# Attention followed by a two-layer MLP on one core: the MLP in two phases, with seven products in both GEMMs

## The chip, the cores and the metric

One core of one Trainium2 chip runs the whole program. The metric is device time in microseconds (us) of one execution; the kernel before has a median of 611.99 us over 3 runs (611.94 to 612.11).

The engines are named as in the profile: PE is TensorE (PEld its weight loads), DVE is VectorE, ACT is ScalarE, POOL is GpSimd, SP is SyncE, which issues most DMAs. PSUM is the memory that PE writes, in eight banks; SBUF is the other on-chip memory; DRAM is off the core.

## What is computed

```python
def _attn_ref(q, k, v):                      # q, k, v: (4, 12, 448, 64) float32
    scores = (1.0 / np.sqrt(64)) * np.matmul(q, k.transpose(0, 1, 3, 2))
    scores = np.where(np.triu(np.ones((448, 448), dtype=bool), k=1), -1e9, scores)
    attn = np.exp(scores - scores.max(-1, keepdims=True))
    return np.matmul(attn / (attn.sum(-1, keepdims=True) + 1e-9), v)

def _moe_ref(x, w_in, w_out, alpha):         # x: the 1792 tokens x 768 of attention
    h = x @ w_in                             # w_in 768 x 2048, float64
    g = np.maximum(h, 0.0) + alpha * np.minimum(h, 0.0)
    return (g @ w_out).astype(np.float32)    # w_out 2048 x 768, float64
```

The two weight matrices arrive as float64. The kernel reads them as pairs of 32-bit words and makes float32 values of them on the chip ("decode"). To keep float32 accuracy on PE, every GEMM operand is split into a high part (a cast to the fp32r type) and a low part (value minus high part), and each product is three matmuls: high by high, high by low, low by high.

## The kernel before, in words

**Attention (0 to about 147 us).** 24 pairs of heads go through a software pipeline; `ORDER` (line 38) lists the steps of one round and how many rounds each lags behind. PE does scores, transposes of the probabilities and the product with v. Decoding for the first group of the MLP is put into the rounds by the table `EARLY` (line 25). The output of each pair is split into a high part, which stays in SBUF (`xw`, `xp`), and a low part, which is stored in DRAM (`lows`, line 184) and loaded again whenever a GEMM step needs it (`load_low`, line 666).

**MLP (about 147 us to the end).** The 2048 hidden features are worked off in 8 groups `g` of 256 (two chunks of 128), the tokens in two blocks `bp` of 2 x 384 and 2 x 512; a (group, block) is a "quad". For each quad the first GEMM makes four PSUM tiles (2 chunks x 2 halves of the tokens). In group 0 that is 12 plain steps of 6 matmuls. In the other groups (`STEPS`, line 642) 4 of the 6 chunks of the inner dimension 768 go through a Strassen-Winograd scheme with 7 products in place of 8 (P1 to P7; sums S1 to S4 of weight blocks, T1 to T4 of token blocks), and the last 2 chunks are added plainly (LX, LY, LZ, LW): 11 steps of 6 matmuls (`h_mms`, line 686; the matmul is line 694). Then `h_act` (line 727) applies the activation, `g_hi` and `g_lo` (lines 748, 755) split the result, and `o_part` (line 783; matmul line 793) does the second GEMM for the same quad at once, plainly: for each tile of 128 tokens and each half of 384 output columns 6 matmuls into one bank, which DVE adds to an accumulator in SBUF (line 798). The second GEMM of quad q-1 is interleaved with the first GEMM of quad q. PE's stream alternates between both GEMMs, so that whatever one waits for, the other covers.

**Decode, per piece of 128 x 384 values** (64 pieces: 32 of w_in, 32 of w_out): ACT absolute value (line 251), POOL clamp (254), four DVE operations (257, 261, 264, 265), POOL add (268). Weight sums S1 to S4 are line 273, casts to the high part lines 295 and 325, low parts on POOL lines 299 and 328.

**What sets the order.** Each engine runs its instructions in program order. The order around the GEMMs is written out by hand in the tables `FIRST`, `SECOND`, `CYCLE` and `LATER` (lines 46 to 115), `PER` (line 117) and `low_calls` (line 935). SP issues all loads of pieces and low parts in order.

## Time and profile before

| | |
|---|---|
| median of 3 runs | 611.99 us |
| span of the profiled execution, first to last instruction | 609.8 us |
| what lies around the span (median less span; the page shows no time of its own for that execution) | 2.2 us |
| PE busy | 603.9 us, 99% |
| DVE, POOL, ACT busy | 507.1, 391.9, 284.5 us |
| instructions | 10958 |
| bytes moved by DMA | 120.40 MB |

How to read it: "busy" is the time in which an engine executed, including time in which an executing instruction was held up inside it. Matmuls overlap in the pipeline, so the mean duration of one matmul is longer than the distance from one to the next; the distance is read from the chain of work, which merges runs of matmuls. "PEclk" is the granted TensorE clock; 9 in the page and 1.00 in a table of stretches are full speed, the 2.4 GHz level.

### The profile page before, as it was taken

To read this page: it belongs to the slowest core of one execution; us is meant where nothing else is said; L and a number is where in the kernel's file an instruction comes from. 1 tells how busy PE (TensorE), PEld (TensorE's weight loads), DVE (VectorE), ACT (ScalarE), POOL (GpSimd) and SP (SyncE) were. 2 spreads that over 40 slices of the span, in tenths; PEclk is the share of its full clock that TensorE was granted. 3 is DMA by queue.
4 is the path that set the end of the run, shared out by engine and by line. 5 is a ranking of instruction groups with operands and counts; after the bars stand their busy time and mean duration, and the time that the engine had idled before them with its cause. 6 is when DMAs were issued, how large, how long until landed. Compare 5 with 4: busy or idle time off the path is not lost.

```text
span 609.8 us, 10958 instructions
## 1 busy us (share of the span) xinstructions
PE 603.9 (99%) x3533; PEld 528.3 (87%) x3533; DVE 507.1 (83%) x1123; ACT 284.5 (47%) x781; POOL 391.9 (64%) x531
## 2 busy tenths in 40 slices
PE   8999999999999999999999999999999999999997
PEld 4676767667879999999999899999999998999897
DVE  5999999998977778988897889878897978896364
ACT  6989989897656743333232313232332323231110
POOL 7766687867485669756874776487568747762120
PEclk9999999999999999999999999999999999999999
DMA  7765477644885598657747756576577467554825
GB/s 171 215 182 160 135 208 221 194 130 121 288 293 155 146 311 264 195 165 229 230 155 228 233 173 205 184 251 194 164 235 231 156 219 238 166 179 118 273 104 181
DMA packets 88105, 120.40 MB, mean 197 GB/s; under 512 B 12400, under 2 KB 66000, under 8 KB 88048
## 3 DMA queue, kind: packets, MB, share of 16 engines
q1 hardware_dynamic: 87008, 117.97, 62.0%
q0 software_dynamic: 576, 1.18, 0.8%
q10 hardware_dynamic: 464, 0.56, 0.3%
q8 instruction: 28, 0.46, 0.3%
q14 instruction: 29, 0.24, 0.1%
HBM read 105.00 MB, written 14.68 MB: 196 GB/s over the span
## 4 chain that ended last, share of the span: by engine, by line
PE 97%; DMA 1%; DVE 1%; POOL 0%; issue 0%; ACT 0%; POOLq 0%; DVEq 0%
PE o L793 38%; PE heldY L694 11%; PE heldX L694 8%; PE a L500 7%; PE pt L481 7%; PE s L425 6%; PE heldZ L694 6%; PE s L417 3%; PE heldW L694 3%; PE h_V L694 3%; PE h_Y L694 1%; PE h_X L694 1%; PE h_W L694 1%; PE h_Z L694 1%; DMA lo_T<-low_T 1%; PE warm L346 1%
## 5 line engine op out<-in xcount | busy, mean ns | idle before, releaser
L798 DVE TENSOR_TENSOR acc<-o,acc 128x384 f32<-128x384 f32 (+1 forms) x197 | 107.6, 550 | 64.1 <-PE o L793 63.4
L406 POOL TENSOR_SCALAR p<-p,rs 128x128 f32<-128x128 f32 (+3 forms) x164 | 81.2, 518 | 36.5 <-ACT ptf L402 22.0
L452 ACT ACTIVATE p<-s,nm 128x256 f32<-128x256 f32 (+3 forms) x168 | 81.9, 496 | 11.5 <-DVE nm L437 10.0
L437 DVE CUSTOM_DVE_ANT_0 s<-s,mask 128x128 f32<-128x128 f32 (+3 forms) x168 | 71.1, 481 | 9.1 <-PE s L425 5.2
L793 PE MATMUL o<-wo,g_Z 128*128 128x384 f32 (+1 forms) x339 | 76.9, 334 | 0.0
L793 PE MATMUL o<-wo,g_W 128*128 128x384 f32 (+1 forms) x339 | 76.7, 334 | 0.0
L793 PE MATMUL o<-wo,g_X 128*128 128x384 f32 x336 | 76.7, 336 | 0.0
L793 PE MATMUL o<-wo,g_Y 128*128 128x384 f32 x336 | 76.5, 335 | 0.0
L793 PEld LDWEIGHTS o<-wo,g_X 128*128 128x128 f32 x336 | 60.3, 188 | 2.0
L793 PEld LDWEIGHTS o<-wo,g_Z 128*128 128x128 f32 x339 | 60.5, 188 | 1.2
L793 PEld LDWEIGHTS o<-wo,g_W 128*128 128x128 f32 x339 | 60.3, 188 | 0.0
L793 PEld LDWEIGHTS o<-wo,g_Y 128*128 128x128 f32 x336 | 60.1, 188 | 0.0
L481 PEld LDWEIGHTS pt<-ident,p 128*128 128x128 f32 x384 | 43.3, 140 | 12.1 <-issue 7.7
L500 PEld LDWEIGHTS a<-ptf,v 128*64 128x64 f32 x384 | 25.4, 136 | 30.8 <-issue 11.2
L268 POOL TENSOR_TENSOR y_o<-y_o,x_o 128x384 f32<-128x384 f32 x32 | 33.4, 1045 | 25.9 <-DVE x_o L265 24.0
L481 PE MATMUL pt<-ident,p 128*128 128x128 f32 x384 | 47.1, 274 | 1.1 <-POOL p L406 1.0
L500 PE MATMUL a<-ptf,v 128*64 128x448 f32 (+3 forms) x384 | 46.8, 386 | 0.0
L268 POOL TENSOR_TENSOR y_i<-y_i,x_i 128x384 f32<-128x384 f32 x32 | 33.1, 1034 | 21.1 <-DVE x_i L265 18.7
L402 ACT ACTIVATE ptf<-pt 128x512 f32<-128x512 f32 (+1 forms) x71 | 37.4, 570 | 3.9 <-PE pt L481 3.8
L425 PE MATMUL s<-kr,qr 64*128 64x384 f32 (+2 forms) x288 | 38.7, 398 | 0.0
L753 ACT ACTIVATE g_Y<-t_Y 128x384 fp32r<-128x384 f32 (+1 forms) x16 | 9.3, 579 | 59.9 <-DVE t_Y L744 59.9
L254 POOL TENSOR_SCALAR x_i<-x_i 128x384 f32<-128x384 f32 x32 | 18.1, 567 | 29.3 <-ACT x_i L251 26.7
(189 smaller groups left out, 1360.1 us busy)
## 6 DMA issues: line engine op xcount, KB each, us to landing
lo_T<-low_T SPq DMA_DIRECT2D x28, 512.0 KB, 5.0
lo_B<-low_B SPq DMA_DIRECT2D x25, 512.0 KB, 4.8
raw_i<-in_moe_w_in_dram SPq DMA_DIRECT2D x32, 384.0 KB, 3.8
raw_o<-in_moe_w_out_dram SPq DMA_DIRECT2D x32, 384.0 KB, 3.7
lo_T<-low_T SPq DMA_DIRECT2D x28, 384.0 KB, 4.0
lo_B<-low_B SPq DMA_DIRECT2D x25, 384.0 KB, 4.0
lo_N<-low_N SPq DMA_DIRECT2D x16, 512.0 KB, 5.3
lo_N<-low_N SPq DMA_DIRECT2D x16, 384.0 KB, 4.3
```

The lines of the kernel that those rows point to most:

```text
L268: nc.gpsimd.tensor_tensor(out=y, in0=y, in1=xf, op=ALU.add)
L402: eng.activation(out, x, AF.Copy, scale=side)
L406: eng.tensor_scalar(out=out, in0=x, scalar1=side, scalar2=1.0, op0=ALU.mult, op1=ALU.mult)
L417: nc.tensor.matmul(ps, qd[p % 3], T["k", p], start=True, stop=True)
L425: nc.tensor.matmul(ps[:, o : o + lim], T["q", p][half(j), i * QP : (i + 1) * QP], T["k", p][half(j), :lim], start=(o == 0), stop=(n > 0 or ...
L437: nc.vector.tensor_tensor_reduce(out=t, in0=t, in1=masks[1] if i == NQ else masks[0][:, (NQ - 1 - i) * QP :], scale=-SCALE, scalar=MOST_F3 ...
L452: nc.scalar.activation(T["p", p, i][:, j, : t.shape[1]], t, AF.Exp, scale=-1.0, bias=T.pop(("nm", p, i, j)), accum_out=T["sm", p][:, z : z ...
L481: nc.tensor.transpose(ps[:, j - js[0], c], t[:, j, c * QP : (c + 1) * QP], T["ident"])
L500: nc.tensor.matmul(out[half(j), c * QP :], vs[b % 2][:, hp, c, j], x[:, c * QP : S], start=(c == 0), stop=(c == NQ),)
L694: nc.tensor.matmul(ps, w[:, u, k * P : (k + 1) * P], x, start=(first and i == 0), stop=(i == len(mms) - 1), skip_group_check=True,)
L793: nc.tensor.matmul(ps, x, w, start=(i == 0), stop=(i == 3 * GC - 1))
L798: nc.vector.tensor_tensor(out=a[:, cols], in0=ps, in1=a[:, cols], op=ALU.add)
```

## The change

The MLP is rewritten; attention keeps its rounds. What it does:

- **First GEMM for all tokens, then the second.** The activated result g (2048 x 1792 float32) is stored in DRAM (`gd`), and so is decoded w_out (`wd`). The second phase loads both back.
- **Seven products on all of both.** The first GEMM splits 768 into 2 x 3 chunks: 7 steps of 9 matmuls of 448 columns for each of 8 groups and 2 halves of the tokens, 1008 matmuls. The second pairs 4 chunks of the hidden dimension (`Q`, 4 of them) with 7 tiles `t` of 2 x 128 tokens: 28 tiles `q`, each 7 steps of 6 matmuls of 384 columns, 1176 matmuls. Before, there were 534 of 384 and 534 of 512 columns, and 1344 of 384.
- **Token operands stay in SBUF,** high and low parts. For tokens of the first half they are made during attention; for the second half T1 to T4 and B11 are kept or stored in float32, B21 and B22 come back from DRAM, and 18 casts and 18 subtractions (128 x 448) behind attention make their parts.
- **Decode with two DVE operations in place of four,** and one ACT operation more: ACT makes an integer of the low word, POOL adds integers.
- **In phase two** each tile needs 4 sums, 7 casts and 7 low parts of g (128 x 256), and each `Q` 8 sums, 14 casts and 14 low parts of w_out (128 x 384). The four output tiles are built by `ofork`, `keep`, `oz`, `evX`, `w22`, `evZ`, `evY`, and in `Q` 1 to 3 `e22`: on DVE 3 additions or copies from PSUM in `Q` 0 and 6 in the others, on ACT 4 and 2.
- **The order of both phases** is no table any more: a planner (`Plan`) lists the jobs with engines, assumed durations (`US`), room in buffers and due times, plays them through in Python when the program is built, and emits them in the order of their planned starts. Jobs marked "DVE|POOL" go to whichever is idle then, the first named first. On the chip each engine still runs its list in order.
- The last steps of group 0 stand in attention's tail: six steps of 9 matmuls, where before there were 14 of 6.

Core of the diff (the planner's loop, attention and the code of the removed tables left out):

```diff
+US = {
+    "abs": 0.56, "int": 0.56, "clamp": 0.62, "bits": 0.68, "add": 1.06, "cast": 0.53, "sum": {"DVE": 0.85, "POOL": 1.06}, "lo": {"DVE": 0.85, "POOL": 1.1},
+    "copy": 0.56, "psum": 0.66, "relu": 0.56, "act": 0.66, "step1": 1.8, "step2": 1.04, "issue": 0.35,
+    "out": 0.56, "take": 0.58, "gcast": 0.42, "gsum": {"DVE": 0.55, "POOL": 0.82},
+    "glo": {"DVE": 0.55, "POOL": 0.85},
+}
+LOAD, STORE = 4.0, 3.0
...
+STEPS = ["P1", "P5", "P6", "P2", "P7", "P3", "P4"]
+STEP = {
+    "P1": ("A11", "B11", "Y"), "P5": ("S1", "T1", "V"), "P6": ("S2", "T2", "Y"), "P2": ("A12", "B21", "X"),
+    "P7": ("S3", "T3", "Y"), "P3": ("S4", "B22", "Z"), "P4": ("A22", "T4", "Y"),
+}
...
+    def p_int(key):
+        ys[key] = rooms["y"].take()
...
+        nc.scalar.activation(ys[key].bitcast(I32), parts_of(key)[0], AF.Copy, scale=2.0**-29)
...
+    def p_shift(key):
+        x = xs[key].bitcast(I32)
+        ts(out=x, in0=x, scalar1=3, scalar2=0x3FFFFFF8, op0=ALU.logical_shift_left, op1=ALU.bitwise_and)
...
+    def p_add(key):
+        y, x = ys[key].bitcast(I32), xs[key].bitcast(I32)
+        nc.gpsimd.tensor_tensor(out=y, in0=y, in1=x, op=ALU.add)
...
+        mms = [m for k in range(KW) for m in ((0, k, xh), (1, k, xh))] + [(0, k, xl) for k in range(KW)]
+        for i, (u, k, x) in enumerate(mms):
+            nc.tensor.matmul(
+                ps, w[:, u, k * P : (k + 1) * P], x[:, k],
+                start=(st in ("P1", "P5") and i == 0), stop=(i == len(mms) - 1), skip_group_check=True,
             )
...
+    def h_relu(g, b, role):
+        t = tt[g, b, role] = rooms["t"].take()
+        nc.scalar.activation(t, bank_of(g, b, role), AF.Relu, scale=-1.0)
...
+        stt(out=t, in0=t, scalar=om[:, f : f + 1], in1=bank_of(g, b, role), op0=ALU.mult, op1=ALU.add)
...
+        nc.sync.dma_start(out=gd[f // 4][:, f % 4, n, b * S : (b + 1) * S], in_=t)
...
+                    job(("xh", nm, k), "ACT", "cast", lambda nm=nm, k=k: t_hi(1, nm, k, nc.scalar), of)
+                    job(("x", 1, nm, k), "DVE|POOL", "lo", lambda e, nm=nm, k=k: t_lo(1, nm, k, e), [("xh", nm, k)])
...
+        half_end = pl.named["P", NG - 1, 0, "P4"]
+        half_end["give"] += ["w"] * 14 + ["gset"] * 2 + ["wf"]
...
+            eng.tensor_tensor(out=g_of(q, nm), in0=g_of(q, x), in1=g_of(q, y), op=op)
...
+            nc.scalar.activation(gset[q][:, LEFT.index(nm), 0], g_of(q, nm), AF.Copy)
...
+            eng.tensor_tensor(out=t[:, 1], in0=g_of(q, nm), in1=t[:, 0], op=ALU.subtract)
...
+            for u in range(2):
+                x, w = gset[q][:, LEFT.index(an)], wo[Q, u, bn]
+                mms += [(x[:, h, u], w[:, l]) for h, l in ((0, 0), (0, 1), (1, 0))]
...
+        def o_plus(out, q, role, x):
+            nc.vector.tensor_tensor(out=out, in0=o_bank(q, role), in1=x, op=ALU.add)
...
+                job(
+                    ("gsum", q, nm), "DVE|POOL", "gsum", lambda e, nm=nm: g_sum(q, nm, e),
+                    [("gl", q)] + [("gsum", q, x) for x in of] + first, "gs" if nm == "S1" else "",
+                )
...
+                    ("glo", q, nm), "POOL|DVE", "glo", lambda e, nm=nm: g_lo(q, nm, e), [("gcast", q, nm)] + later,
...
+        for i in range(NQT * NTT // 2):
+            for st in STEPS:
+                for b in range(2):
+                    o_jobs(2 * i + b, st)
```

## Rows read from the trace of the kernel before

**Rows 1.** The page: busy time of each engine, and the chain that ended last

```profile
PE 603.9 (99%) x3533; PEld 528.3 (87%) x3533; DVE 507.1 (83%) x1123; ACT 284.5 (47%) x781; POOL 391.9 (64%) x531
...
PE 97%; DMA 1%; DVE 1%; POOL 0%; issue 0%; ACT 0%; POOLq 0%; DVEq 0%
```

**Rows 2.** Stretches: PE, PEld, DVE, ACT, POOL busy us (x instructions); clock, DMA share, GB/s

```profile
113.00:144.00 31.00, 31.00 (x234) 20.69 (x232) 29.25 (x109) 29.33 (x99) 22.62 (x47) 1.00 0.39 119
216.00:328.00 112.00, 112.00 (x602) 106.44 (x601) 97.42 (x161) 37.52 (x85) 78.76 (x89) 1.00 0.68 217
```

**Rows 3.** The chain in order of time: start us, us, what

```profile
183.40 20.83 PE o L793 x120
...
217.10 2.10 PE heldY L694 x12
...
240.11 2.75 PE heldY L694 x12
```

**Rows 4.** Groups by line and shape: xcount | busy us, mean ns | idle, releaser

```profile
L798 DVE TENSOR_TENSOR acc<-o,acc 128x384 f32<-128x384 f32 x195 | 106.9, 552 | 63.7 <-PE o L793 63.1
...
L328 POOL TENSOR_TENSOR wo<-y_o,wo 128x384 fp32r<-128x384 f32 x32 | 34.9, 1092 | 0.0
...
L268 POOL TENSOR_TENSOR y_i<-y_i,x_i 128x384 f32<-128x384 f32 x32 | 33.1, 1034 | 21.1 <-DVE x_i L265 18.7 <-PE heldX L694 2.5
...
L299 POOL TENSOR_TENSOR wi_A<-y_i,wi_A 128x256 fp32r<-128x256 f32 x25 | 21.1, 844 | 0.0
...
L261 DVE SCALAR_TENSOR_TENSOR y_i<-raw_i,x_i 128x384 int32<-128x384 int32 x32 | 20.3, 635 | 0.4
L257 DVE TENSOR_SCALAR x_i<-x_i 128x384 int32<-128x384 int32 x32 | 20.3, 634 | 6.6 <-POOL x_i L254 6.6
...
L254 POOL TENSOR_SCALAR x_i<-x_i 128x384 f32<-128x384 f32 x32 | 18.1, 567 | 29.3 <-ACT x_i L251 26.7 <-PE heldY L694 2.2
...
L251 ACT ACTIVATE x_i<-raw_i 128x384 f32<-128x384 f32 x32 | 17.8, 555 | 29.2 <-DMA raw_i<-in_moe_w_in_dram 29.1
...
L325 ACT ACTIVATE wo<-y_o 128x384 fp32r<-128x384 f32 x32 | 15.5, 511 | 0.8 <-PE a L500 0.8
...
L295 ACT ACTIVATE wi_A<-y_i 128x256 fp32r<-128x256 f32 x25 | 10.3, 412 | 0.3 <-POOL y_i L268 0.3
...
L402 ACT ACTIVATE xw<-acc 128x448 fp32r<-128x448 f32 x11 | 5.8, 582 | 0.0
...
L744 DVE SCALAR_TENSOR_TENSOR t_X<-heldX,t_X 128x512 f32<-128x512 f32 x7 | 4.8, 692 | 0.2
...
L725 ACT ACTIVATE heldY<-heldX 128x512 f32<-128x512 f32 x7 | 4.1, 581 | 26.4 <-PE heldX L694 26.4
...
L744 DVE SCALAR_TENSOR_TENSOR t_X<-heldX,t_X 128x384 f32<-128x384 f32 x7 | 3.9, 557 | 0.2
```

**Rows 5.** DVE in order of time, 300 to 330 us: start us, us, instruction

```profile
299.99 0.56 DVE L798 TENSOR_TENSOR acc<-o,acc 128x384 f32<-128x384 f32 x1 [1.13 <-PE o L793]
300.46 1.30 DVE L265 SCALAR_TENSOR_TENSOR x_o<-raw_o,x_o 128x384 f32<-128x384 uint32 x1
...
322.12 0.56 DVE L265 SCALAR_TENSOR_TENSOR x_o<-raw_o,x_o 128x384 f32<-128x384 uint32 x1
```

**Rows 6.** DVE in order of time, 180 to 184 us

```profile
182.83 0.42 DVE L273 TENSOR_TENSOR S<-y_i,y_i 128x256 f32<-128x256 f32 x1
```

**Rows 7.** POOL in order of time, 300 to 330 us

```profile
300.06 1.29 POOL L758 TENSOR_TENSOR g_X<-t_X,g_X 128x512 fp32r<-128x512 f32 x1 [0.31 <-ACT g_X L753]
...
304.11 0.73 POOL L299 TENSOR_TENSOR wi_A<-y_i,wi_A 128x256 fp32r<-128x256 f32 x1
```

**Rows 8.** DMA issues: xcount, KB each, median us from issue to landing

```profile
lo_T<-low_T SPq DMA_DIRECT2D x28, 512.0 KB, 5.0
...
raw_i<-in_moe_w_in_dram SPq DMA_DIRECT2D x32, 384.0 KB, 3.8
...
low_B<-low_B SPq DMA_DIRECT2D x16, 224.0 KB, 3.5
```

More of the change, by code (lines that the diff above doesn't have):

```diff
@@ L419, in scores @@
             return
-        banks = [bank(f"s_{p}_{n}_{j}") for j in range(2)]
+        banks = [bank("s", p, n, j, uses=2 - n) for j in range(2)]
         o = 0
@@ new lines, in t_lo, with t_both, t_four @@
+    def t_lo(h, nm, k, eng):
+        eng.tensor_tensor(
+            out=XL[h][nm][:, k], in0=x_f32(h, nm, k), in1=XH[h][nm][:, k], op=ALU.subtract
+        )
+    t_his, t_los, u_both = (
+        iter([(h, nm, k) for nm in names for k in range(KW)]) for h, names in ((0, TF), (0, TF), (1, ["B11"]))
+    )
+    t_fours = iter(range(KW))
+    def t_both(*x):
+        t_hi(*x, nc.scalar)
+        t_lo(*x, nc.vector)
+    def t_four():
+        k = next(t_fours)
+        nc.gpsimd.tensor_tensor(out=TF["T4"][:, k], in0=TF["T4"][:, k], in1=TF["T2"][:, k], op=ALU.subtract)
@@ L924, in scores_done, with pool @@
+    bits = {}
+    def pool(stack, name, side="left"):
+        return stack.enter_context(tc.tile_pool(name=name, bufs=1, side=side, reuse_waits="tile"))
+    more_s, late_s = ExitStack(), ExitStack()
     def scores_done():
         att_a.close()
-        for nm, n in (("t", 3), ("low", 4)):
-            gp[nm] = pool("m_" + nm, n, "right")
-        load_low(4)
+        more = pool(more_s, "more", "right")
+        more.tile([P, 8], F32, name="padr")
+        b11 = more.tile([P, 2, KW, S], F32R, name="b11")
+        wir = more.tile([P, 4, 2, NH], F32R, name="wir")
+        XH[1]["B11"], XL[1]["B11"] = b11[:, 0], b11[:, 1]
+        nc.sync.dma_start(out=b11[:, 1].bitcast(F32), in_=xd["B11"])
+        for i in range(4):
+            rooms["wi"].give(wir[:, i])
@@ new lines, with piece_jobs @@
+        left = {nm: len(x.free) for nm, x in rooms.items()}
+        pl = Plan(left, done)
+        job = pl.job
+        def piece_jobs(key, before, by=1e9):
+            k = ("add", key)
+            if k in done:
+                return
+            if ("load", key) not in done:
+                job(("load", key), "SP", "issue", lambda: p_load(key), (), "raw", lag=LOAD, by=by, behind=[("load", before)])
+            job(("abs", key), "ACT", "abs", lambda: p_abs(key), [("load", key)], "x", by=by, behind=[("abs", before)])
+            job(("clamp", key), "POOL", "clamp", lambda: p_clamp(key), [("abs", key)], by=by)
+            job(("int", key), "ACT", "int", lambda: p_int(key), [("load", key)], "y", by=by, behind=[("int", before)])
+            job(("shift", key), "DVE", "bits", lambda: p_shift(key), [("clamp", key)], by=by)
+            job(("sign", key), "DVE", "bits", lambda: p_sign(key), [("shift", key), ("int", key)], give=["raw"], by=by)
+            job(("add", key), "POOL", "add", lambda: p_add(key), [("sign", key), ("int", key)], give=["x"], by=by)
+            if key[0] == "o":
+                job(("store", key), "SP", "issue", lambda: p_store(key), [("add", key)], give=["y"], lag=STORE, by=by)
@@ new lines, with __init__, __getitem__ @@
+        wl_last = []
+        class At:
+            def __init__(self, t):
+                self.t = t
+            def __getitem__(self, i):
+                return acc[self.t][i]
+        for Q in range(NQT):
+            w_jobs(Q)
+        for q in range(NQT * NTT):
+            g_jobs(q)
+        for i in range(NQT * NTT // 2):
+            for st in STEPS:
+                for b in range(2):
+                    o_jobs(2 * i + b, st)
+        pl.run({"DVE": nc.vector, "POOL": nc.gpsimd})
```

1271 lines of the change are left out of this document (682 added, 589 removed), and 16 rows, old and new, of tables (EARLY, PER, STEP).

## The prediction

> **What bounds the kernel now.** I read the page's busy times and chain first, then the table of stretches. PE is busy for 603.9 of 609.8 us and the chain that ended last is PE for 97% [rows 1]. In the steady MLP PE has no gap at all, 112.00 of 112.00 us, at clock 1.00, the 2.4 GHz level [rows 2]. So the time is PE's work, and a change pays only by taking matmul columns away, and loses whatever makes PE wait. The same stretch shows who could do that: DVE is busy 97.4 of 112 us (87%), POOL 78.8 (70%), ACT only 37.5 [rows 2]. In the last part of attention ACT is the full one, 29.33 of 31 us [rows 2].
>
> **PE's work.** The chain gives the distance between matmuls: 2.10/12 = 0.175 us at 384 columns, 2.75/12 = 0.229 at 512, 20.83/120 = 0.1736 in the second GEMM [rows 3]. 448 columns lie midway: 0.202. First GEMM: before 534 x (0.175 + 0.229) = 215.8 us, after 1008 x 0.202 = 203.7. Second: before 1344 x 0.1736 = 233.3, after 1176 x 0.1736 = 204.1. Together 41.3 us go. Attention's own matmuls stay. With the median 611.99 (2.2 us over the profiled span of 609.8; I take those 2.2 as unchanged) a PE without new gaps gives **570.7 us**. The rest of this part is the gaps.
>
> **What a DVE or POOL operation costs beside the other.** This price decides, so I looked at single instructions. DVE's multiplication of two SBUF operands (128x384) took 0.56 us alone but 1.30 when it began 0.4 us into a POOL operation of 1.29, and ended 0.4 after it [rows 5, 7]. An accumulation from PSUM beside the same POOL operation took its usual 0.56 [rows 5, 7], and its mean over 195 is 0.552 [rows 4]. So DVE operations that read SBUF twice wait for POOL's, and those on PSUM do not. In means: the two decode operations on DVE cost 0.63 each [rows 4]. A POOL low part of 128x256 took 0.73 alone and 0.844 in the mean; one of 128x384 1.092 [rows 4, 7]. The Trainium skill states the rule behind it (GPSIMD Engine Reference, section 8, Key points): GpSimd shares its SBUF interfaces with VectorE and contends with VectorE instructions that have two SBUF inputs. The rows agree; by that rule alone this change, which moves work onto exactly such operations, should lose something, and it names no price.
>
> **Phase two, per tile (the critical sum).** PE: 42 x 0.1736 = 7.29 us. ACT: 7 casts x 0.412, 2 casts of w_out x 0.511, 2 to 4 copies from PSUM of about 0.5 [rows 4] make 4.9 to 5.9 us: covered. DVE in `Q` 1 to 3: 6 operations from PSUM x 0.552 = 3.31. DVE and POOL share 11 operations of 128x256 and, in `Q` 0 to 2, 22/7 = 3.1 of 128x384 for the next `Q`. On DVE a 128x256 one costs between 0.42, alone [rows 6], and about 1.0 (0.42 plus most of a POOL operation); I take 0.67, since the decode operations' means lie about 0.2 above their times alone and POOL will be fuller than its 70%. If POOL takes the w_out work (3.1 x 1.09 = 3.4) and 4.7 of the others (x 0.844 = 4.0), it needs 7.4 us, and DVE 3.31 + 6.3 x 0.67 = 7.5. Both stand at PE's 7.29 already, and both waits grow when both are full: the shared operations alone take 3.1 x 1.09 + 4.7 x 0.73 + 6.3 x 0.42 = 9.5 us that overlap only in their starts. I take 7.9 us in `Q` 1 and 2 (14 tiles): +8 us. `Q` 0 has three operations fewer on DVE, `Q` 3 no w_out to prepare: 0. Ends: 0, and 9.3 us (every DVE operation behind one of POOL) in 21 tiles, +42.
>
> **Phase one.** Decode left for it is 59 pieces. DVE: 59 x 2 x 0.635 = 75, 96 operations from PSUM at 0.625 (between 0.557 and 0.692) = 60, and about 31 of the 95 sums and low parts at 0.85 = 26: 161 us. POOL: 59 x (0.567 + 1.034) = 94, and 64 x 1.09 = 70: 164. The integer add I price as the float one, 1.034 (ends 0.84 and 1.29, the nearest POOL operations of 256 and of 512). ACT: 118 decode operations x 0.555 (the integer conversion priced as the absolute value, same shape; ends 0.41 and 0.58, the cast of 256 and the one of 448), 67 casts at 0.51 to 0.58, 94 PSUM operations at 0.55: about 153 [rows 4, 7]. All below PE's 204, so nothing bounds it on the average, but the planner puts decode early and the sums that release PE's next step (Z, V and the activations) queue behind it on DVE. I take +3; ends 0 and 12. The loads of pieces land 3.8 us after issue [rows 8] with three buffers; a piece holds one for some 8 us, so 2.7 us per piece, 159 us for 59: hidden, with little room. SP issues in order: 64 stores of g and 32 of w_out now stand between those loads, each waiting for DVE or POOL, and the next piece's load waits behind it; planned starts keep that apart, so I price it at 0 and leave it in the end of 12.
>
> **Start of phase one.** Before, 14 steps of group 0 covered attention's tail; now six longer ones do, and the second token half is not ready. Behind the last pair B21 goes out (3.5 us, [rows 8]) and comes back (3.8), then cast 0.58 and low part about 0.7: with semaphores some 10 us. PE has only P4, P1, P5, P6 to run, 4 x 9 x 0.202 = 7.3. That is +3. ACT has 18 casts x 0.58 = 10.5 plus forks, activations and the decode of group 1, some 20 us of work in a window of 17: +2. So +5, ends 1 and 10. **Attention:** ACT takes on 8 copies of 0.55 and some 4 more decode and cast operations, about 6 us against some 7 free (1.67 in the 31 us shown [rows 2], over the 127 us of full rounds); DVE loses more than it gains. +1, ends 0 and 6.
>
> **Hand-over between the phases.** Half of the last group, 63 x 0.202 = 12.7 us, is the time to prepare 14 casts, 14 low parts and 8 sums of w_out and two tiles of g. That is 44 shared operations, which POOL and DVE together get through in about 27 us; PE has 12.7 + 14.6 us of work up to the end of the first two tiles, but needs the first parts early. +4, ends 0 and 12. The last tile's stores end as before.
>
> **The sum:** 570.7 + 1 + 5 + 3 + 4 + 8 = 591.7, so **592 us**, 3.3% faster. DMA traffic doesn't enter: low parts are no longer reloaded, against a g load of 512 KB per 7.3 us, like the one that landed in 5.0 us [rows 8], with three buffers.
>
> **Rivals.** (1) *Everything hides.* The mean prices leave DVE and POOL just at PE's rate in the second phase, and buffers for four prepared tiles smooth it. Only the start (5) and a little remain: about 577 us. Against it: no slack on two engines at once. (2) *DVE and POOL take turns.* This is the slower side: in phase two, `Q` 0 to 2, each shared DVE operation finds a POOL operation running, costs like the 1.30 row, and a tile takes 9.3 us: 21 x 2 = 42 us, with the other terms 570.7 + 13 + 42 = 626. It decides against the change from 8.6 us per tile on (28 us lost beside the 13). For it: in rows 5 and 7 the wait is complete, and the planner adds both engines up as if they were independent. Against it: half of DVE's work there reads PSUM, which doesn't wait, and the steady stretch before runs 87% and 70% without a gap. (3) *The start and the hand-over are worse than sized:* 10 and 12 in place of 5 and 4, 605 us; still faster.
>
> **Chances.** Forecast (582 to 602) 0.50, rival 1 0.23, rival 3 0.07, rival 2 and what lies between it and break-even 0.20. From no change a measurement of this kernel tells about 0.2% (1.2 us). Faster by over that: 0.79; within: 0.02; slower: 0.19. The range leaves out the upper half of rival 2 and the tail of rival 1: 575 to 614.
>
> **What would show it.** PE's chain: 0.202 per matmul of the first GEMM, 7.3 us per tile of the second where nothing waits. In the stretches of phase two, PE below 100% in `Q` 1 and 2 and near 100% in `Q` 3 would show the shared-operation term right; DVE's 128x256 subtractions with a mean near 0.67. PE waiting on B21's low part about 7 us behind attention shows the start term. Wrong would be: a steady second phase without gaps (rival 1), DVE means above 0.9 (rival 2), phase one losing more than 10 us, or a granted clock below 1.00 in either phase, of which no row here gives a case.

## The result, and the profile after

The changed kernel takes 616.29 us (median of 4 runs, 615.32 to 617.2), the kernel before 612.05 in the same comparison (611.94 to 612.51). The ratio is 1.0072, 95% interval 1.006 to 1.0084: **0.7% slower**, where 592 us and faster were predicted. The profiled execution took 616.45 us for a span of 614.6, so 1.8 us lie around it (2.2 before).

The profile page after, busy times and the chain that ended last (for [rows 1]):

```profile
PE 581.2 (95%) x3300; PEld 500.2 (81%) x3300; DVE 528.8 (86%) x1093; ACT 395.6 (64%) x1058; POOL 475.1 (77%) x609
...
PE 16%; DVE 11%; POOL 2%; issue 2%; ACT 0%; DVEq 0%; POOLq 0%; ACTq 0%
```

PE's busy time fell by 22.7 us against 603.9 before, although a half-clock matmul now counts twice, and 33 us of the span are idle. The chain, all PE before, now stops following PE: walked back from the end it soon runs on DVE too, and it breaks off in the middle (its shares sum to 31%).

The stretches after (columns as in [rows 2]; the first two are those of [rows 2]):

```profile
113.00:144.00 31.00, 30.04 (x216) 20.07 (x216) 26.93 (x104) 26.98 (x89) 22.21 (x42) 1.00 0.31 90
216.00:328.00 112.00, 111.03 (x544) 101.72 (x543) 101.40 (x145) 72.22 (x153) 91.52 (x100) 1.00 0.75 237
172.00:200.00 28.00, 19.13 (x81) 15.98 (x78) 23.93 (x27) 19.65 (x42) 22.99 (x21) 0.88 0.45 147
200.00:285.00 85.00, 85.00 (x418) 78.30 (x417) 76.36 (x111) 55.55 (x118) 69.98 (x75) 1.00 0.74 235
285.00:335.00 50.00, 48.06 (x234) 43.44 (x232) 42.67 (x64) 29.57 (x63) 35.92 (x42) 1.00 0.74 238
335.00:385.00 50.00, 41.17 (x177) 36.30 (x178) 38.06 (x54) 25.73 (x55) 34.99 (x37) 0.90 0.63 203
385.00:410.00 25.00, 22.60 (x116) 20.53 (x115) 20.19 (x30) 17.18 (x43) 20.07 (x20) 1.00 0.44 144
410.00:460.00 50.00, 47.52 (x265) 45.24 (x264) 49.90 (x74) 33.02 (x87) 47.49 (x51) 1.00 0.40 117
460.00:585.00 125.00, 123.82 (x709) 122.47 (x709) 122.72 (x201) 68.40 (x182) 119.11 (x137) 1.00 0.35 105
```

Read the second column first. Where phase one is settled (200 to 285) PE has no gap. It loses 9 us behind attention (172 to 200), 2 between 285 and 335, 9 between 335 and 385, and some 5 around the phases' hand-over (385 to 460). From 460 on it runs within 1% of full, with DVE busy 98% and POOL 95%. The clock column is below 1.00 in two places, both beside gaps.

From the starts of the matmuls (line 357 for phase one, 1136 for phase two) each part can be timed, a group of phase one being 126 matmuls, a quarter of phase two 294:

| part | without gaps | measured | gap | predicted |
|---|---|---|---|---|
| attention (A.V products of the last pairs, against before) | | 6.2 later | 6.2 | 1 |
| group 0's last step of the first half to group 1 (72 matmuls) | 14.6 | 26.25 | 11.65 | 5 |
| groups 1 to 7 | 7 x 25.45 = 178.2 | 25.7 x 4, 27.05, 33.67, 32.92 = 196.5 | 18.3 | 3 |
| first quarter of phase two | 51.0 | 57.84 | 6.8 | 4 |
| second to fourth quarter | 153.1 | 52.11, 52.84, 51.22 = 156.2 | 3.1 | 8 |

The gaps sum to 46 us in place of 21. With the 570.7 of PE's work that makes 616.7, within half a microsecond of the measured times. So PE's work came out as computed (1.8 us of the groups' gap is pitch, the distance from one matmul to the next: 25.7 us a group where nothing waits, against 25.45), and the error is in the gaps. Of attention's 6.2, 0.9 is there at the first pair already (its A.V products start at 16.2 us against 15.3); runs with the same attention code start it anywhere from 15.3 to 17.7.

PE's longest waits after (waited-for line, us in total, times, longest), then the two longest waits of the DMA queue for loads of weight pieces:

```profile
PE bank L357 <- DVE bank L371: 6.2, 2, 5.6
PE bank L357 <- POOL wie L339: 3.4, 2, 1.8
PE bank L357 <- POOL wir L339: 3.2, 2, 2.2
PE bank L357 <- ACT wie L336: 3.2, 1, 3.2
```

```profile
SPq L254 <- DVE dec L282: 34.6, 12, 6.6
SPq L258 <- DVE dec L282: 29.6, 16, 10.7
```

One wait of 5.6 us is for line 371, VectorE's addition in PSUM that makes Z. The three others (9.8 us, all between 333 and 376 us) are for weights of the late groups: casts (336) and low parts (339). Lines 254 and 258 load a piece of w_in and of w_out; 28 times they stood, 64 us in all, until the sign operation (282) had freed a raw buffer; for the third one, which the program cuts from `tf`, they stood 7 times and 9.6 us more. The late weights begin there.

What a shared operation costs, DVE and then POOL in order of time in the stretch before the 5.6 us wait ended:

```profile
183.98 1.57 DVE L627 TENSOR_TENSOR x2l<-x2l,x2h 128x448 fp32r<-128x448 f32 x1
185.47 0.92 DVE L627 TENSOR_TENSOR x2l<-tf,x2h 128x448 fp32r<-128x448 f32 x1
186.32 1.48 DVE L307 TENSOR_TENSOR dec<-dec 128x384 f32<-128x384 f32 x1
187.72 1.29 DVE L278 TENSOR_SCALAR dec<-dec 128x384 int32<-128x384 int32 x1
188.93 1.55 DVE L627 TENSOR_TENSOR x2l<-tf,x2h 128x448 fp32r<-128x448 f32 x1
190.40 0.55 DVE L282 SCALAR_TENSOR_TENSOR dec<-dec 128x384 int32<-128x384 int32 x1
190.87 0.61 DVE L627 TENSOR_TENSOR x2l<-x2l,x2h 128x448 fp32r<-128x448 f32 x1
191.40 0.62 DVE L371 TENSOR_TENSOR bank<-bank,tf 128x448 f32<-128x448 f32 x1
```

```profile
182.04 3.02 POOL L627 TENSOR_TENSOR x2l<-x2l,x2h 128x448 fp32r<-128x448 f32 x2
185.04 0.87 POOL L274 TENSOR_SCALAR dec<-dec 128x384 f32<-128x384 f32 x1
185.89 1.49 POOL L627 TENSOR_TENSOR x2l<-tf,x2h 128x448 fp32r<-128x448 f32 x1
187.34 2.65 POOL L627 TENSOR_TENSOR x2l<-x2l,x2h 128x448 fp32r<-128x448 f32 x2
191.02 1.31 POOL L289 TENSOR_TENSOR dec<-dec 128x384 int32<-128x384 int32 x1 [1.03 <-DVE dec L282]
```

In these rows, while POOL is busy, every DVE operation on SBUF takes 0.92 to 1.57 us and ends some 0.2 to 0.5 us after a POOL instruction has ended (185.55 behind 185.04, 187.80 behind 187.38). When POOL stands idle from 189.99, the same low part takes 0.61 and the sign operation 0.55. POOL's short clamp (274) takes 0.87 in turn, where the kernel before had 0.567 in the mean [rows 4]. The two take turns. The Trainium skill (SBUF — State Buffer, section "SBUF: two separate sides") states this as an exclusive lock that the first of the two holds for its whole instruction; these rows agree, and the addition from PSUM (line 371, 0.62 here, 0.625 in the mean) stands outside it, as they show too.

Groups on DVE in phase one (200 to 397 us), then in phase two (397 to 585), columns as in [rows 4]:

```profile
L282 DVE SCALAR_TENSOR_TENSOR dec<-dec 128x384 int32<-128x384 int32 x38 | 32.2, 849 | 0.2
...
L371 DVE TENSOR_TENSOR bank<-bank,tf 128x448 f32<-128x448 f32 x28 | 17.4, 625 | 7.1 <-PE bank L357 5.7 <-ACT dec L271 1.3
...
L339 DVE TENSOR_TENSOR wir<-dec,wir 128x384 fp32r<-128x384 f32 x7 | 7.2, 1037 | 0.0
```

```profile
L1149 DVE TENSOR_TENSOR acc<-bank,acc 128x384 f32<-128x384 f32 x49 | 25.1, 544 | 0.3
...
L1118 DVE TENSOR_TENSOR gset<-dec,gset 128x256 fp32r<-128x256 f32 x19 | 14.4, 761 | 0.1
...
L1106 DVE TENSOR_TENSOR dec<-tf 128x256 f32<-128x256 f32 x14 | 10.9, 776 | 0.0
```

### The profile page after: what moved, and what is told of

It reads as the page before. It is cut to its first block, busy times and chain, and to the rows that moved or that the text cites. A ratio compares the mean times of both kernels' runs of the same rounds, so it can differ in the third digit from the quotient of the medians.

```text
span 614.6 us, 11020 instructions
## 1 busy us (share of the span) xinstructions
PE 581.2 (95%) x3300; PEld 500.2 (81%) x3300; DVE 528.8 (86%) x1093; ACT 395.6 (64%) x1058; POOL 475.1 (77%) x609
## 5 line engine op out<-in xcount | busy, mean ns | idle before, releaser
L514 ACT ACTIVATE p<-bank,nm 128x256 f32<-128x256 f32 (+3 forms) x168 | 81.9, 499 | 17.0 <-DVE nm L499 13.0
L499 DVE CUSTOM_DVE_ANT_0 bank<-bank,mask 128x128 f32<-128x128 f32 (+3 forms) x168 | 71.2, 481 | 10.1 <-PE bank L487 6.4
L1136 PE MATMUL bank<-x1h,x1l 128*128 128x384 f32 x318 | 61.9, 338 | 3.8 <-ACT x1l L1114 1.8
L1136 PE MATMUL bank<-x1h,gset 128*128 128x384 f32 x312 | 61.8, 336 | 1.4 <-ACT tf L1244 0.7
L1136 PEld LDWEIGHTS bank<-x1h,x1l 128*128 128x128 f32 x318 | 55.3, 188 | 6.1 <-ACT x1l L1114 2.5
L1136 PEld LDWEIGHTS bank<-x1h,gset 128*128 128x128 f32 x312 | 54.5, 188 | 2.7 <-ACT tf L1244 1.0
L544 PEld LDWEIGHTS bank<-ident,p 128*128 128x128 f32 x384 | 43.1, 140 | 14.6 <-POOL p L468 7.1
L357 PE MATMUL bank<-x2h,wir 128*128 128x448 f32 x192 | 46.9, 381 | 5.6 <-DVE bank L371 5.6
L357 PE MATMUL bank<-x1h,wir 128*128 128x448 f32 x192 | 46.5, 377 | 4.7 <-POOL wir L339 3.2
L544 PE MATMUL bank<-ident,p 128*128 128x128 f32 x384 | 48.0, 275 | 2.3 <-POOL p L468 2.2
L564 PE MATMUL bank<-ptf,v 128*64 128x448 f32 (+3 forms) x384 | 46.8, 386 | 0.0
L289 POOL TENSOR_TENSOR dec<-dec 128x384 int32<-128x384 int32 x27 | 29.4, 1087 | 16.2 <-DVE dec L282 14.6
```

The source lines that it names most:

```text
L289: nc.gpsimd.tensor_tensor(out=y, in0=y, in1=x, op=ALU.add)
L357: nc.tensor.matmul(ps, w[:, u, k * P : (k + 1) * P], x[:, k], start=(st in ("P1", "P5") and i == 0), stop=(i == len(mms) - 1), skip_group_ ...
L499: nc.vector.tensor_tensor_reduce(out=t, in0=t, in1=masks[1] if i == NQ else masks[0][:, (NQ - 1 - i) * QP :], scale=-SCALE, scalar=MOST_F3 ...
L514: nc.scalar.activation(T["p", p, i][:, j, : t.shape[1]], t, AF.Exp, scale=-1.0, bias=T.pop(("nm", p, i, j)), accum_out=T["sm", p][:, z : z ...
L544: nc.tensor.transpose(ps[:, j - js[0], c], t[:, j, c * QP : (c + 1) * QP], T["ident"])
L564: nc.tensor.matmul(out[half(j), c * QP :], vs[b % 2][:, hp, c, j], x[:, c * QP : S], start=(c == 0), stop=(c == NQ),)
```

## The experiments

Seventeen runs of sixteen kernels (e11 and e17 are the same); each time is set against the kernel before on the same chip, 611.5 to 612.4 us. All but e17 are single executions, and the four of the changed kernel lie 1.9 us apart, so a difference of 1 us in a total tells nothing. Where an edit changes the jobs, the planner makes a new order for all that follows, so that parts far from the edit move too. "Stretch" is the one of 26.25 us above, "groups" the sum of groups 1 to 7 (196.5), Q0 the first quarter of phase two (57.84).

### Phase one: too few buffers, or too much work?

**e1_no_wout_arith.** The pieces of w_out are loaded and other data of the same size is stored.

```diff
         def piece_jobs(key, before, by=1e9):
...
+            if key[0] == "o":
+                job(("store", key), "SP", "issue", lambda: p_pass(key), [("load", key)], give=["raw"], lag=STORE, by=by)
+                return
```

> The 32 pieces of w_out are still loaded and something is still stored for them, but their arithmetic (2 ACT, 2 POOL, 2 DVE operations each) is left out. If phase one loses its time because DVE and POOL have too much shared work, groups 6 and 7 run without waits and the time falls by 16 to 20 us, to about 597 to 600. If it is the chain of each w_in piece (load, buffers, due times) that is late, groups 6 and 7 keep most of their 16 us and the time stays above 610.

596.33 us, 20.0 less, as the first reading had it: 16.1 of them in the groups. Every group took 25.7 to 25.85 us, the stretch 25.58, Q0 57.33. The stretches of this run:

```profile
200.00:285.00 85.00, 85.00 (x417) 77.78 (x416) 51.95 (x81) 44.37 (x92) 46.42 (x50) 1.00 0.81 260
285.00:335.00 50.00, 50.00 (x247) 46.02 (x246) 27.68 (x44) 25.00 (x52) 28.55 (x31) 1.00 0.82 264
```

Without the decoding of w_out phase one has no gap from 200 us on, so 16 of the groups' 18.3 us hang on that work and not on the first GEMM itself; the other 2 are pitch. It also frees raw buffers sooner, so this run alone doesn't part buffers from work.

**e2_more_raw.** Two of the eight y buffers (decoded pieces) become a fourth raw buffer (loaded pieces, before decoding).

```diff
-            (("T2", "T4"), [("raw", t24[:, : 2 * NH].bitcast(I32))]
-             + [("y", t24[:, i * NH : (i + 1) * NH]) for i in range(2, 6)]
+            (("T2", "T4"), [("raw", t24[:, i * NH : (i + 2) * NH].bitcast(I32)) for i in (0, 2)]
+             + [("y", t24[:, i * NH : (i + 1) * NH]) for i in range(4, 6)]
```

> Two of the eight buffers for decoded pieces become a fourth buffer for loaded ones. If the rate of loads (three buffers, each held about 9 us) makes the pieces of groups 6 and 7 late, the time falls by 8 to 15 us, to 601 to 608, and SP waits less for DVE's sign operation than 64 us. If the shared operations are the bound, it stays within 3 us of 616.

607.17 us: 9 us less than the changed kernel, with the same work (6.6 in the groups, 2.1 in phase two). Groups 6 and 7 fell from 33.67 and 32.92 to 26.04 and 26.71; the groups sum to 189.9, and 3.41 us at half clock remain there in place of 10.24. The expectation's second sign did not come: SP's waits for the sign operation did not fall. The rows of e2, for both places that buffers are cut from:

```profile
SPq L258 <- DVE dec L282: 35.3, 19, 10.7
SPq L254 <- DVE dec L282: 24.9, 15, 6.6
...
SPq L254 <- DVE tf L282: 11.1, 6, 3.2
SPq L258 <- DVE tf L282: 7.9, 6, 2.6
```

That is 79 us in 46 waits, against 74 in 35 in the changed kernel. Pieces pass faster (the last load is issued at 346 us in place of 362), but each holds its buffer longer, 11.6 us in the mean in place of 9.8 (from issue to the end of the sign operation, over the 57 loads from 177 us on). The fourth buffer raised the pace and filled up as well. Its stretches:

```profile
200.00:285.00 85.00, 83.63 (x408) 75.84 (x407) 81.35 (x110) 55.39 (x118) 77.83 (x84) 1.00 0.75 235
285.00:335.00 50.00, 46.00 (x215) 41.15 (x215) 48.23 (x66) 32.98 (x72) 45.27 (x49) 0.97 0.78 254
335.00:389.00 54.00, 53.34 (x260) 48.29 (x259) 41.67 (x57) 29.89 (x68) 37.27 (x39) 1.00 0.60 191
```

The late weights are gone, and a smaller loss has come forward: between 285 and 335 DVE is busy 96% and POOL 91%, and PE misses 4 us. So some 7 of the 18 us are the buffers; of the 11.7 left 1.8 are pitch, and the rest stands beside a full DVE and POOL.

**e5_due_early.** Pieces of w_in due 8 us earlier, buffers unchanged.

```diff
-(26.0 if g < NG - 1 else 30.0)
+(34.0 if g < NG - 1 else 38.0)
```

> The pieces of w_in for groups 1 to 7 are given due times 8 us earlier; number of buffers as in the changed kernel. Theory (three raw buffers set the rate at which pieces can pass, not their due times): the same number of pieces has to go through the same three buffers by group 7, so the late groups stay late; groups 5, 6 and 7 together stay above 90 us (93.6 in the changed kernel) and the time stays within 612 to 619. Rival (the due times are simply too late): groups 5 to 7 fall to 26 to 27 us each, together below 81, and the time to 600 to 605.

615.05 us. Groups 5 and 6 fell to 25.90 and 25.81, 7 stayed at 32.32, and Q0 rose to 67.01. The sum of 5 to 7 is 84.0, in neither range, but the total is the theory's: the groups won 9.6 us and Q0 lost 9.2. The pieces that are moved forward push the w_out pieces back, and their lateness is paid at the hand-over. The due times only say who waits.

**e8_real_prices.** The planner's table gets the durations measured beside POOL, on top of e2's buffer.

```diff
-    ... "bits": 0.68, ... "sum": {"DVE": 0.85, "POOL": 1.06}, "lo": {"DVE": 0.85, "POOL": 1.1},
+    ... "bits": 0.78, ... "sum": {"DVE": 1.05, "POOL": 1.15}, "lo": {"DVE": 1.1, "POOL": 1.2},
...
-    "out": 0.56, "take": 0.58, "gcast": 0.42, "gsum": {"DVE": 0.55, "POOL": 0.82},
-    "glo": {"DVE": 0.55, "POOL": 0.85},
+    "out": 0.56, "take": 0.58, "gcast": 0.42, "gsum": {"DVE": 0.8, "POOL": 0.9},
+    "glo": {"DVE": 0.77, "POOL": 0.88},
```

> The fourth raw buffer as in e2_more_raw, and the planner is given the durations that the trace of the changed kernel shows beside GpSimd (sums on VectorE 1.05 in place of 0.85, low parts 1.1, decode operations 0.78, low parts of g 0.77, and so on), so the order of the instructions on VectorE and GpSimd is made for those. Theory (VectorE's additions in PSUM wait because the planner queues more shared operations ahead of them than there is time for): groups 1 to 7 together fall from 189.9 us in e2_more_raw to 181 to 185 and the time to 598 to 603. Rival (the waits come from the engines being full, whatever the order): groups 1 to 7 stay at 187 to 193, the second phase is not shorter, and the time stays at 605 to 611.

615.95 us; the theory fell, and the time lies above the rival's range too. The groups sum to 189.0, no better than e2's 189.9, and phase two is 9 us longer than in e2 (Q0 59.97, third quarter 56.25). Truer prices for single operations didn't help a plan that still counts the two engines as independent.

**e10_later_wout** and **e16_combo_due.** Both with e2's buffer and e7's order (below). e10 spreads w_out's pieces over 14 us more; e16 has w_in's due 4 us earlier, with e11's buffers.

```diff
-((NG - 1) * PER - 40.0) / len(outs)
+((NG - 1) * PER - 26.0) / len(outs)
```

```diff
-(26.0 if g < NG - 1 else 30.0)
+(30.0 if g < NG - 1 else 34.0)
```

> The fourth raw buffer of e2_more_raw, the attention order of e7_att_order, and the due times of the w_out pieces stretched to 26 us before the end of phase one in place of 40. Theory (the waits left in groups 2 to 5, 10 us over their work in e2_more_raw, come from decode crowding VectorE and GpSimd beside the steps): groups 1 to 7 fall from 189.9 us to 185 to 187, the hand-over (first quarter of phase two, 57.7) rises by 0 to 3, attention gives 2.5, the time is 600 to 604. Rival (the crowding only moves): groups 1 to 7 and the first quarter together stay within 1.5 us of 247.6, the time is 604 to 606, 2.5 under e2_more_raw by attention alone.

> e11_v_slot with the w_in pieces due 4 us earlier. Theory (with the fourth raw buffer the rate suffices and the due times matter): groups 1 to 7, 190.9 us in e11_v_slot, fall to 184 to 188 and the hand-over stays within 2 us of 57.5: time 599 to 603. Rival (VectorE and GpSimd are full in all of phase one, and the loss moves): 603 to 606.

607.71 us (groups 190.3, Q0 59.51) and 605.78 (188.0, 60.02). Neither theory held; e16 came out as its rival, e10 worse than both. Groups and Q0 together are 249.8 and 248.0 us against 247.6 in e2: the loss moves between the phases and doesn't shrink, which speaks for full engines and against lateness. That it is their turns, and not their work alone, is argued from the rows of single instructions; no run lifts the turns by themselves.

### The stretch behind attention

**e3_x2_dve.** All 18 low parts of the second half on DVE.

```diff
-job(("x", 1, nm, k), "DVE|POOL", "lo", ...
+job(("x", 1, nm, k), "DVE|DVE", "lo", ...
```

> The 18 low parts behind attention all on DVE. If DVE and POOL take turns on them, one engine does them at 0.62 in place of the mean 1.33, and the start of phase one loses about 6 us less: about 610. If the two engines really share that work, DVE alone takes longer and the time rises to 618 to 622.

618.23 us; stretch 26.08. The theory's 6 us didn't come, since its price didn't: on DVE the low parts took up to 1.43 us, twelve of the eighteen 1.42 in the median, because POOL had other work beside them (it was busy for 8.52 of the 12 us from 180, against 10.97). The total fits the rival's range, but its loss lies elsewhere (Q0 62.59).

**e9_no_x2_lows** and **e12_no_x2_casts** left out the 18 low parts or the 18 casts and loaded other data in their place.

> The 18 low parts of the second token half behind attention are left out (other data is loaded in their place for the four T blocks, the two B blocks keep what was loaded); their 18 casts on ScalarE stay. Theory (the stretch from group 0's last step of the first half to group 1 is set by the shared work of VectorE and GpSimd): it falls from 26.25 us to 17 to 20, without a stretch at half clock. Rival (ScalarE's casts and copies set it): it stays at 23 to 26. The time falls by the same amount, so 607 to 610 or 614 to 617; the late groups 6 and 7 don't change.

> The changed kernel with the 18 casts of the second token half behind attention left out (other data is loaded in their place); the 18 low parts stay. Beside e9_no_x2_lows, which took the low parts away and gained 1.6 us of the stretch. Theory (ScalarE's queue of casts, copies and decode operations sets the stretch): it falls from 26.25 us to 17 to 21. Rival (each of the three engines is full in it, so taking work from one of them leaves the others): 23 to 26. The late groups 6 and 7 don't change.

619.9 us with a stretch of 24.64, and 630.42 with 33.24. Both were spoilt by those loads: in e9 ACT stands 4.56 us for B21's load, which is behind them, and PE 3.0 us for the cast of it; in e12 PE waits 2.1 us for such a load itself. They settle nothing, and were repeated without loads.

**e14_no_lows_clean** and **e15_no_casts_clean** multiply tiles of the first half instead (in e14 for the T blocks; for the B blocks what was loaded).

```diff
-job(("x", 1, nm, k), "DVE|POOL", "lo", lambda e, nm=nm, k=k: t_lo(1, nm, k, e), [("xh", nm, k)])
+job(("x", 1, nm, k), "SP|SP", "none", lambda e: None, [("xh", nm, k)])
...
-            XH[1][nm], XL[1][nm] = x2h[:, i], x2l[:, i]
+            XH[1][nm], XL[1][nm] = x2h[:, i], XL[0][nm] if nm in TF else x2l[:, i]
```

```diff
-job(("xh", nm, k), "ACT", "cast", lambda nm=nm, k=k: t_hi(1, nm, k, nc.scalar), of)
+job(("xh", nm, k), "SP", "none", lambda: None, of)
...
-            XH[1][nm], XL[1][nm] = x2h[:, i], x2l[:, i]
+            XH[1][nm], XL[1][nm] = XH[0][nm], x2l[:, i]
```

> As e9_no_x2_lows, but nothing is loaded in their place, since those loads stood ahead of B21's: the 12 low parts of the T blocks and the 6 of the B blocks of the second half are left out (for T, the first half's low parts are multiplied instead). Theory (the shared operations of VectorE and GpSimd set the stretch from group 0's last step of the first half to group 1): 26.25 us fall to 17 to 20. Rival (ScalarE's casts and copies set it): 23 to 26.

> As e12_no_x2_casts, without the loads, for which TensorE waited there: the 18 casts of the second half are left out (the first half's high parts are multiplied instead), the 18 low parts stay. Theory (shared operations of VectorE and GpSimd set the stretch): it stays at 23 to 26. Rival (ScalarE sets it): 17 to 20.

Without low parts the stretch is 20.26 us, 6.0 less (just outside the range named); without casts 25.20, 1.05 less, which is little beside the 25.5 to 26.4 us of the stretch in the changed kernel and the eight others that leave its work alone. The totals (617.26 and 623.37) are no measure of it: groups 5 to 7 and Q0 were longer in both (Q0 62.26 and 62.70), which wasn't followed up, and e15's attention began 1.5 us later. Two stretches, of the changed kernel and then of e14:

```profile
180.00:186.00 6.00, 4.20 (x18) 3.37 (x19) 6.00 (x5) 4.93 (x11) 6.00 (x6) 1.00 0.44 139
186.00:192.00 6.00, 0.43 (x3) 0.05 (x1) 6.00 (x8) 4.72 (x11) 4.97 (x4) 0.92 0.01 2
```

```profile
180.00:186.00 6.00, 3.04 (x15) 2.44 (x13) 1.32 (x3) 3.75 (x9) 1.06 (x2) 1.00 0.42 141
186.00:192.00 6.00, 5.30 (x18) 4.81 (x19) 2.21 (x4) 4.50 (x11) 3.44 (x4) 0.72 0.44 132
```

In the changed kernel DVE is full for these 12 us and POOL for 11 of them, while PE stands for over 7. So the stretch is mainly set by the shared low parts on DVE and POOL, and ScalarE's casts cost 1 us at most. The 5.7 us still over 14.6 in e14 (a wait of 3.7 for Z's addition, and half clock) were not parted further.

**e11_v_slot.** e2's buffer, e7's order, and the two buffers of the kept P5 result cut from T1's place.

```diff
-            (("T1", "T3"), [("t", t13[:, i * S : (i + 1) * S]) for i in range(4)]
-             + [("v", t13[:, i * S : (i + 1) * S]) for i in range(4, 6)]),
+            (("T1",), [("v", t13[:, i * S : (i + 1) * S]) for i in range(2)] + [("t", t13[:, 2 * S : 3 * S])]),
+            (("T3",), [("t", t13[:, i * S : (i + 1) * S]) for i in range(3, 6)]),
```

> The fourth raw buffer and the attention order, and the two buffers of the kept P5 result are cut from T1's place, which is read out before T3's, so that the copy that Z's addition needs doesn't wait for T3's low parts. Theory (that wait is part of the 5.7 us wait for Z's addition): the stretch from group 0's last step of the first half to group 1 falls from 25.5 us to 22.5 to 24.5. Rival (Z's addition waits for VectorE's queue and ScalarE's, not for the buffer): 25 to 26.5. Time 601 to 604 or 604 to 606.

604.28 us, stretch 24.80, and 25.47 when the same kernel ran again (e17), against 25.5 with e7's order (e7, e10): the buffer is worth 0 to 0.7 us. The total is what e2's buffer and e7's order give together.

**e13_fill.** 13 useless matmuls ahead of the step that waits for Z.

```diff
         done_with("wi", wi, (g, an))
+        for _ in range(13 if (g, b, st) == (0, 1, "P2") else 0):
+            nc.tensor.matmul(bank_of(g, b, "Z"), w[:, 0, :P], XH[0]["B11"][:, 0], start=True, stop=True, skip_group_check=True)
```

> The fourth raw buffer and the attention order, and 13 matmuls without use (448 columns, 2.65 us at the full clock) issued to TensorE ahead of the step that waits for Z's addition, so that it stands still for some 3 us in place of 5.7. Theory (the half clock of 6.83 us behind that wait follows from TensorE's standing still): the half-clock stretch is gone, and the stretch to group 1 falls from 25.5 us to 22 to 23. Rival (the clock falls for the same time whatever those matmuls do, or Z's addition is later for them): 25 to 28 us, with the 6.83 us at half clock as before.

605.53 us. PE around the wait in e7 (no filling and no fourth buffer), then in e13:

```profile
183.34 0.77 PE L357 MATMUL bank<-x2l,wir 128*128 128x448 f32 x3
189.77 2.61 PE L357 MATMUL bank<-x2h,wir 128*128 128x448 f32 x6 [5.65 <-DVE bank L371]
```

```profile
184.38 2.83 PE L363 MATMUL bank<-x1h,wir 128*128 128x448 f32 x13
190.23 1.79 PE L357 MATMUL bank<-x2h,wir 128*128 128x448 f32 x6 [3.02 <-DVE bank L373]
```

PE stood 3.02 us in place of 5.65, and the clock still fell, for 3.41 us in place of 6.83; but it now fell while PE had work, where half of the 6.83 lay in the wait. The stretch is 25.33 against 25.47: nothing gained, and both the theory and the rival missed.

### Attention

**e4_att_pool.** The sums S and the low parts of T in attention on POOL in place of DVE.

```diff
-fns.append(lambda: t_lo(*next(t_los), nc.vector))
+fns.append(lambda: t_lo(*next(t_los), nc.gpsimd))
...
-"S": a_sum}[kind]
+"S": lambda g, nm: a_sum(g, nm, nc.gpsimd)}[kind]
```

> In attention the four sums S and the twelve low parts of T go from DVE to POOL. If the longer rounds (6.4 to 7.6 us in place of 6.08) come from DVE's chain between the row sums of one pair and the maxima of the next, the rounds return to about 6.1 and the time falls by 4 to 6 us, to 610 to 612. If POOL's normalizations are the longest link, the rounds grow and the time rises by 2 to 8 us.

616.92 us, and attention was 1.8 us later at pairs 20 and 22 (145.4 and 160.1 against 143.6 and 158.3). Starts scatter, so the better measure is from the first pair's A.V products to those of pair 20: 129.5 us here, 127.4 to 127.7 in the changed kernel and the ten other runs with its attention. Relieving DVE didn't help and loading POOL cost 2 us there; the total rose by 0.6, less than either reading had it.

**e7_att_order.** POOL's integer additions one pair later; its sums of T4 spread over pairs 18, 20, 22.

```diff
-    14: "C:2 sub:A11 D:2:1 4 h", 15: "D:2:1 l +:2 LD A:3 4 h", 16: "l C:3 D:3:1 S:S1 4 h", ...
+    14: "+:1 C:2 sub:A11 D:2:1 h", 15: "D:2:1 l LD A:3 h", 16: "+:2 l C:3 D:3:1 h", 17: "D:3:1 l S:S1 LD h",
```

> In attention, GpSimd's integer additions of the decode are issued one pair later than now and three of its sums of T4 are moved from pairs 14 to 16 to pairs 18, 20 and 22. Theory (GpSimd stands waiting for the sign operation of VectorE at the head of its queue, and the normalisations of attention behind it are late): the A.V products of pair 20 start at 139 to 141 us in place of 143.6 and those of pair 22 at 154 to 156 in place of 158.3; group 0's last step of the first token half moves from 174.1 to 170 to 172; the time falls by 2 to 4 us. Rival (ScalarE and VectorE are full in these pairs and set the pace): pair 20 stays within 0.6 us of 143.6 and the time within 1.5 us of the changed kernel's.

614.81 us, 1.5 less, short of the 2 to 4 named. Pair 20 starts at 141.1 and pair 22 at 155.7, 2.5 us earlier; group 0's last step of the first half at 171.5. Of the 2.5, 0.6 is an earlier start: from the first pair's products to pair 20's it is 125.4 us (125.3 to 125.8 in the five other runs with this order) against 127.4, and 122.1 in the kernel before. POOL in the changed kernel, from 136 us:

```profile
136.56 1.00 POOL L289 TENSOR_TENSOR dec<-dec 128x384 int32<-128x384 int32 x1 [3.38 <-DVE dec L282]
137.54 0.56 POOL L468 TENSOR_SCALAR x1h<-tf 128x448 fp32r<-128x448 f32 x1
138.08 3.35 POOL L468 TENSOR_SCALAR p<-p,rs 128x128 f32<-128x128 f32 x7
```

The addition (289) stood 3.38 us for DVE's sign operation, and behind it in POOL's queue were a copy of T and seven normalisations that attention needed. PE's waits for the normalisations (line 544 on 468) are 2.2 us in 4 times in the changed kernel and 0.8 in one here. So the new order is worth 2.0 of the 5.4 us that attention lost by pair 20; whether the additions or the sums of T4 gave it was not parted, and the rest was not settled.

### The hand-over, and the best version

**e18_no_q0_lows.** No low parts of w_out for the first quarter.

```diff
-            eng.tensor_tensor(out=t[:, 1], in0=x, in1=t[:, 0], op=ALU.subtract)
+            if Q:
+                eng.tensor_tensor(out=t[:, 1], in0=x, in1=t[:, 0], op=ALU.subtract)
```

> The changed kernel without the 14 low parts of w_out for the first quarter of phase two (what lies in their place is multiplied). Theory (the hand-over is work that VectorE and GpSimd share, done beside the first tiles): the first quarter falls from 57.84 us to 52 to 54, and the rest of the kernel stays within 1.5 us. Rival (the hand-over waits for loads and for ScalarE's casts of w_out and g): 56.5 to 58.5.

615.16 us, Q0 55.42: 2.4 us less, between the two ranges. The first two tiles now ran without a gap, the first stretch here against PE's 5.96 of 7.20 us from 396.8 on in the changed kernel, but a later stretch paid (PE 11.69 of the 14 us from 410, against 13.29):

```profile
396.00:403.00 7.00, 7.00 (x41) 6.89 (x40) 3.70 (x7) 3.92 (x10) 2.48 (x4) 1.00 0.83 264
403.00:410.00 7.00, 6.97 (x41) 6.60 (x39) 4.61 (x6) 4.29 (x12) 4.35 (x5) 1.00 0.35 106
410.00:424.00 14.00, 11.69 (x66) 11.12 (x65) 12.67 (x22) 10.68 (x31) 12.90 (x15) 1.00 0.45 128
```

Shared work is part of the hand-over; the other 4.4 us were not parted.

**e17_e11_timed.** e11's kernel, timed.

> The kernel of e11_v_slot again, timed: 604 to 605.5 us, a ratio to the kernel before of 0.986 to 0.989, so 1.1 to 1.4% faster than the kernel before and 1.8 to 2.1% faster than the changed one. If its one time was a lucky one: 606 to 609.

604.5 us, median of 4 runs (603.75 to 605.63), ratio to the kernel before 0.988, 95% interval 0.9863 to 0.9896: **1.2% faster than before** and, against 616.29, 1.9% faster than the changed kernel. With one more buffer, two others moved and a shifted order the change pays, though far less than the 41 us of PE's work.

## Why the prediction was wrong

**Right: PE's work.** The matmuls took the pitch computed: 25.71 us for 126 in a settled group (0.204 us, predicted 0.202) and 50.96 for 294 in the last quarter of several runs (0.1733, predicted 0.1736). Hand-over and phase two together, 4 + 8, measured 9.9, which is partly luck: the one was 6.8 and the other 3.1. In the second and third quarter lines 1106 and 1118 cost DVE 0.83 us in the mean (0.67 was taken), and DVE did 24 of the 45 operations on w_out, which the term had given to POOL; but it did only 56 of the 148 operations of 256 columns, 4.0 a tile where 6.3 were supposed. A tile needed 7.4 to 7.5 us where 7.9 was taken.

**Wrong: phase one, +3.** This is the step that failed most: the term measured 18.3 us, 15.3 of the 25 by which the sum missed, and losing more than 10 there had been named as a sign of error. Two of its sentences are wrong.

The first is "2.7 us per piece, 159 us for 59: hidden, with little room". It multiplied a holding time of 8 us, whose parts it doesn't list, by pieces over three buffers, and found 159 us inside 204. In the trace a buffer was held for 9.8 us in the mean: 57 pieces over three buffers make 186 of the 195 us from the first of these loads (177.5) to the last sign operation (372.8), and between 200 and 360 they were taken 99% of the time in the mean. The page shows the load itself as expected (3.7 us, [rows 8] had 3.8), but the buffer goes back only after the sign operation, the last of a chain over ACT, POOL and DVE, each waiting for its turn. A fourth buffer returned 9 us, 6.6 of them in the groups (e2), leaving the arithmetic out 16.1 in the groups (e1); earlier due times only moved the loss (e5). SP's order, which the term priced at 0, was not what held the loads: SP did stand 51.2 us, in 40 waits, until stores of g could go (line 391 on 385), but the buffers were never empty for long.

The second is "nothing bounds it on the average". DVE's and POOL's 161 and 164 of 204 us were taken as independent. As the two take turns, what counts is DVE's part on SBUF, 75 + 26 us by the prediction's own terms, plus POOL's 164: 265 us, more than 204. Those prices hold waits, so the sum is too high, but it says that nothing is free. That the rest of the groups' loss comes from these turns is argued: it stands beside DVE and POOL at 96 and 91% (e2), goes with their work (e1) and only moves when the plan changes (e8, e10, e16).

**Wrong: the start, +5.** The term counted ACT's casts and the trip of B21 through DRAM, and named a wait for B21's low part. That wait didn't come: PE waited for low parts of T1 (1.27 us) and T2 (1.02), ran B21's step without a gap and then stood 5.64 for Z's addition. The 18 low parts were counted among phase one's 95 sums and low parts, but not here, where they stand; beside POOL they cost up to 1.57 us on DVE, and Z's addition stands behind them in its queue. They are worth 6.0 us (e14), the casts at most 1.05 (e15). The other 5.7 stay open.

**Wrong: attention, +1.** "DVE loses more than it gains" was true (26.93 us against 29.25 in the stretch of [rows 2], which now holds somewhat less of the work) and beside the point. POOL's queue wasn't walked: the addition that waits at its head delays seven normalisations. The order without that is worth 2.0 us (e7), 0.9 of the 6.2 is a later start, and the rest stays open.

**Named as a sign of error:** a granted clock below 1.00, "of which no row here gives a case". It came: 17 us at half speed within the MLP (6.83 us from 191, 6.83 from 338, 3.41 from 375), each at a gap. In the first, 15 matmuls that need 3.06 us took 5.77, so 2.7 of the start's 11.65 us are the clock's. In the other two, 24 matmuls that need 4.9 us kept PE busy for 8.6, so some 3.7 of the groups' 18.3 are. It follows the gaps: without those of the late groups it is 1.00 in all of phase one behind the start (e1).

**The rivals.** Rival 2 had the mechanism right, that DVE and POOL take turns, but put it into phase two at 9.3 us a tile. There some 3.3 of DVE's 7.4 us a tile read PSUM and stay outside, most of POOL's operations are the short ones of 256 columns (0.86 to 0.89 in the mean), and a tile took 7.5. The turns decided in phase one and at its start, where the operations are long and something urgent stands behind them. Rival 3 was right on the start (11.65, it had 10) and not on the hand-over (6.8, it had 12); rival 1 failed.
